# Attention with soft cap, then two MLPs, on one core: a pair's products with v are issued one pair earlier, in PSUM banks of their own

## The chip, the core and the metric

The kernel runs on one core of one Trainium2 chip. The metric is the device time of one execution in microseconds; before the change it is 471.43 us, the median of 3 runs (471.33 to 472.37). Five engines with their own instruction streams work side by side: TensorE (PE in the profile; its weight loads are PEld), VectorE (DVE), ScalarE (ACT), GpSimd (POOL) and SyncE (SP, which issues most DMAs). Each runs its own instructions in the order in which they stand and waits on semaphores for the others.

## The reference

```python
batch, n_heads, seq, head_dim = (2, 12, 448, 64)
n_tokens, d_model, d_ff = (896, 768, 2048)      # first MLP; the second has d_ff 1024

def _attn_ref(q, k, v, cap):
    scores = np.matmul(q, k.transpose(0, 1, 3, 2)) / np.sqrt(q.shape[-1])
    scores = cap * np.tanh(scores / cap)
    scores = scores - np.max(scores, axis=-1, keepdims=True)
    attn = np.exp(scores)
    attn = attn / (np.sum(attn, axis=-1, keepdims=True) + 1e-09)
    return np.matmul(attn, v)

def _moe_ref(x, w_in, w_out, s, b):
    r = np.maximum(x @ w_in, 0.0)
    return (s * (r * r) + b) @ w_out

def _moe2_ref(x, w_in, w_out, g_ln):
    h = x @ w_in
    e = np.exp(h - np.max(h, axis=-1, keepdims=True))
    solu = h * (e / (np.sum(e, axis=-1, keepdims=True) + 1e-09))
    ln = layer_norm(solu) * g_ln
    return ln @ w_out
```

The three follow each other: the output of the attention, 896 tokens by 768, is x of the first MLP, and so on.

## The kernel before

The attention treats the 24 heads as 12 pairs, 0 to 11. All work of a pair n has short names, which stand in the program's order too:

- **pk, pq** (`prep`, lines 418 to 453): TensorE transposes the pair's keys and queries into PSUM. DVE copies the keys to `kh` and makes the rest `kl` (L450, L451); for q it is `qh` and `ql` (L438 or, on ACT, L442, and L443). Each operand of a score is thus split in two, and a product of two split operands is three matmuls (`terms`).
- **s** (`scores_by_key`, L469): scores, transposed, keys on the partitions, in four tiles c = 0 to 3 of a pool `ps_s` with two buffers of two banks. Tiles 0 to 2 hold 128 keys of each head, the last one holds the 64 left over of both. ACT takes tanh of each tile into `e` (L474).
- **exps** (`exps_by_key`, L481): ACT, in two halves: tiles 0 and 1, then 2 and 3.
- **c** (`sums_by_key`, `ends_by_key`): POOL adds up the exponentials of a pair in two adds (L490 after the first half, L493 after the second), then DVE adds the last part in two instructions (L499).
- **o** (`products_by_key`, L511): the product with v, 8 plain float32 matmuls in two halves; the first needs the first half of the exponentials, the second half the rest.
- **m** (`values_by_key`, L521): TensorE sums `c` over the partitions; DVE transposes m (`mt`, L528), inverts it, spreads it (L530, L534), and multiplies o by it (`xf`, L539).
- **split_x**: xf is split again into `xh` and `xl`, the operands of the first MLP: on POOL (L548, L552) for pairs 0 to 9, on ACT and DVE (L199, L200) for pairs 10 and 11.

PSUM has eight banks. While the attention runs, `ps_s` has four of them and the other four are the four buffers of a pool `ps_t`, from which pk, pq, o and m of all pairs take turns.

The order is written out by hand: `then(step, ...)` (line 744) holds each step of the loop in lines 770 to 811 behind the one before it on every engine. Step n of the loop puts on TensorE: s of pair n, tiles 0 and 1; o and m of pair n-2; s of pair n, tiles 2 and 3; pk and pq of pair n+2. The steps of `weights.pump` between them convert the first weights of the MLP (`wt_wi`, L218 to L243, on DVE and ACT), so that DVE has such work in the middle of the attention. DMAs have no place in that order: they are issued by SP in the order in which the program has them, and wait there until what they overwrite is free. The keys, queries and values come in groups of four heads, two pairs; group 0's keys and queries are loaded at the very start, then group 1's, then group 0's v.

After the attention the first MLP begins: `in0_fc` and `in448_fc` are its products for the tokens of the first and of the second batch, from x of pairs 0 to 5 and of pairs 6 to 11. A scheduler mixes the first of these products into the end of the attention.

Of the kernel before, what the change touches and what calls it, by code (L numbers as in the profile page):

```python
# [10 lines left out]
F32 = mybir.dt.float32  # L11
# [26 lines left out]
def tile_softcap_attention__relu2__solu(  # L38
# [20 lines left out]
    P = 128  # L59
# [18 lines left out]
    def psum(name, bufs):  # L78
        return tc.tile_pool(name=name, bufs=bufs, space=PSUM, reuse_waits="tile")
# [4 lines left out]
    def by_query(src, b, heads):  # L84
        return src[b, heads].rearrange("h (p c) d -> p h (c d)", c=NC)
# [4 lines left out]
    def zero_by_key(t, by_pair):  # L90
        for par in range(2):
            threes = (slice(D, P), slice(0, D))[par]
            if by_pair:
                nc.gpsimd.memset(t[threes, :, 3:, par], 0.0)
            else:
                nc.gpsimd.memset(t[threes, par::2, 3 * D:], 0.0)
# [42 lines left out]
    for pr in range(2):  # L139
        pair = slice(2 * pr, 2 * pr + 2)  # L140
# [19 lines left out]
    with psum("ps_w", 1) as ps_w:  # L160
        idle = ps_w.tile([P, 512], F32, name="idle")
# [16 lines left out]
    def layers(ctx, general):  # L178
# [197 lines left out]

        att = ExitStack()
        ps_s = att.enter_context(psum("ps_s", 2))
        ps_t = att.enter_context(psum("ps_t", 3 if general else 4))
        ps_a = att.enter_context(psum("ps_a", 1)) if general else None  # L380
        ap_ = att.enter_context(sb("att", side="right"))

# [3 lines left out]
        def load_group(g, names=("k", "q", "v")):  # L386
            b, i = divmod(g, GB)
            heads = slice(4 * i, 4 * i + 4)
            for nm, src in (("k", k), ("q", q), ("v", v)):
                if nm not in names:  # L390
                    continue
                by_key = nm != "q" and not general
                if g == 0 and (nm == "q" or nm == "k" and by_key):
                    nat[nm, g] = first[nm]
                    continue
                by_pair = nm != "v"
                shape = [P, 2, NC, 2, D] if by_pair else [P, 4, NC * D]
                if by_key:
                    if (nm, g % 3) not in kept:
                        kept[nm, g % 3] = ap_.tile(shape, F32, name=f"{nm}n{g % 3}")  # L400
                        zero_by_key(kept[nm, g % 3], by_pair)
                    t = kept[nm, g % 3]
                    load_by_key(t, src, b, heads, by_pair)
                    nat[nm, g] = t
                    continue
                t = ap_.tile(shape, F32, tag=f"{nm}n", name=f"{nm}n{g}", bufs=3)
                if by_pair:
                    t = t[:CP]
                    load_by_query(t, src, b, heads, nc.gpsimd if g < 2 else None)
                else:  # L410
                    t = t[:CP]
                    nc.sync.dma_start(out=t, in_=by_query(src, b, heads))
                nat[nm, g] = t

        split = {}
        st = {}
# [37 lines left out]

        def terms(n):
            (kh, kl), (qh, ql) = split["k", n], split["q", n]
            return (kh, qh), (kh, ql), (kl, qh)

# [42 lines left out]

        def products_by_key(n, half):
            if half == 0:
                st["o", n] = ps_t.tile([P, 512], F32, tag="t", name=f"o{n}")
            vn = nat["v", n // 2]
            o = st["o", n]
            for c in (2 * half, 2 * half + 1):
                for j in range(2):  # L510
                    nc.tensor.matmul(  # L511
                        o[j * D:(j + 1) * D, :S],
                        lhsT=vn[:, 2 * (n % 2) + j, c * D:(c + 1) * D],
                        rhs=st["e", n][:, 2 * c + j if c < 3 else 6, :],
                        start=(c == 0), stop=(c == NC - 1),
                    )
# [142 lines left out]
        for kk in range(KD):  # L659
            for n in range(2):  # L660
                f = slice(n * HALF, (n + 1) * HALF)
# [43 lines left out]
        for _ in prep(0):  # L705
            pass
        load_group(1, ("k", "q"))
        load_group(0, ("v",))
        if general:
            load_group(2, ("k", "q"))  # L710
            load_small()
            load_group(1, ("v",))
        NPR = NH // 2
        preps = {}

        def prep_half(n):
            if n < NPR:
                if n not in preps:
                    preps[n] = prep(n)
                next(preps[n], 0)  # L720

        if general:
            load_group(2, ("v",))
            for n in range(NPR + 2):
                for c in range(NC):
                    i, c2 = 2 * n + c // 2, c % 2
                    if i < NH:
                        scores(i, c2)
                    if 0 <= i - 1 < NH:
                        exps(i - 1, c2)  # L730
                    if 0 <= i - 2 < NH:
                        transposes(i - 2, 2 * c2)
                        transposes(i - 2, 2 * c2 + 1)
                    if c < 2:
                        prep_half(n + 1)
                if n % 2 == 1 and n // 2 + 3 < NG:
                    load_group(n // 2 + 3)
                if n >= 2:
                    values(n - 2)
        else:  # L740
            last = {}
            traced = nc.cur_bb.bb.instructions

            def then(step, *args):
                with ExitStack() as behind:
                    for ins in last.values():
                        behind.enter_context(tc.issue_after(ins))
                    n = len(traced)
                    step(*args)
                for ins in traced[n:]:  # L750
                    if ins.engine in ordered:
                        last[ins.engine] = ins

            ordered = [e.engine for e in (nc.tensor, nc.vector, nc.scalar, nc.gpsimd)]
            xs["x"] = act_tiles("x")
            idle = ps_t.tile([P, 512], F32, tag="t", name="idle2")
            for n in range(6):
                nc.tensor.matmul(idle[:D, :D], lhsT=ones, rhs=ones, start=True, stop=True)
            then(scores_by_key, 0, 0)
            then(scores_by_key, 0, 1)  # L760
            then(prep_half, 1)
            then(prep_half, 1)
            weights.load(0)
            load_group(2, ("k", "q"))
            load_small()
            load_group(1, ("v",))
            load_group(2, ("v",))
            weights.load(1)
            steps = {1: 3, **{n: 1 for n in range(3, NPR - 2)}, NPR - 2: 2, NPR - 1: 3}
            for n in range(NPR + 2):  # L770
                now = n < NPR
                if now and n > 0:
                    then(scores_by_key, n, 0)
                    then(scores_by_key, n, 1)
                if not now:
                    then(weights.pump, 2)
                if n == 1:
                    then(prep_half, 2)
                    then(prep_half, 2)
                    then(ends_by_key, 0)  # L780
                if n >= 2:
                    then(products_by_key, n - 2, 0)
                    then(products_by_key, n - 2, 1)
                    then(values_by_key, n - 2)
                if now:
                    then(exps_by_key, n, 0)
                if n >= NPR:
                    then(split_x, n - 2)
                elif n >= 3:
                    then(split_x, n - 3)  # L790
                if now:
                    then(sums_by_key, n, 0)
                    then(scores_by_key, n, 2)
                    then(scores_by_key, n, 3)
                    then(exps_by_key, n, 1)
                if 1 < n < NPR:
                    then(ends_by_key, n - 1)
                if n > 0:
                    then(prep_half, n + 2)
                    then(prep_half, n + 2)  # L800
                then(weights.pump, steps.get(n, 0))
                if now:
                    then(sums_by_key, n, 1)
                if n == NPR - 1:
                    then(ends_by_key, n)
                if n == NPR - 1:
                    then(split_x, n - 2)
                if n % 2 == 1 and n // 2 + 3 < NG:
                    load_group(n // 2 + 3, ("k", "q"))
                if n % 2 == 1 and 3 <= (n + 3) // 2 < NG:  # L810
                    load_group((n + 3) // 2, ("v",))
# [129 lines left out]
        for b in range(B):  # L941
            for dc in (2, 3):
                pool, tag = (ps_a, "a") if b == 0 else (ps_b, "b")
# [180 lines left out]
```

## Time and profile before

| what | value |
|---|---|
| time, median of 3 runs | 471.43 us (471.33 to 472.37) |
| the profiled execution's own time | 474.06 us |
| its span, from the first to the last instruction | 472.3 us |
| TensorE busy | 461.2 us, 98% of the span |
| VectorE busy | 346.3 us, 73% |
| ScalarE busy | 273.9 us, 58% |
| GpSimd busy | 92.0 us, 19% |
| mean granted TensorE clock | 0.998 of full speed |

The attention takes about the first 110 us of the span, where GpSimd is busy too. A matmul's end is modelled, so a busy TensorE means that its next instruction was not held up, and not that it runs at its peak. The profiled execution's own time is its span and 1.8 us around it; it lies 2.6 us over the median of the runs.

### The profile page before, as it was taken

To read this page: it belongs to the slowest core of one execution; us is meant where nothing else is said; L and a number is where in the kernel's file an instruction comes from. 1 tells how busy PE (TensorE), PEld (TensorE's weight loads), DVE (VectorE), ACT (ScalarE), POOL (GpSimd) and SP (SyncE) were. 2 spreads that over 40 slices of the span, in tenths; PEclk is the share of its full clock that TensorE was granted. 3 is DMA by queue.
4 is the path that set the end of the run, shared out by engine and by line. 5 is a ranking of instruction groups with operands and counts; after the bars stand their busy time and mean duration, and the time that the engine had idled before them with its cause. 6 is when DMAs were issued, how large, how long until landed. Compare 5 with 4: busy or idle time off the path is not lost.

```text
span 472.3 us, 6596 instructions
## 1 busy us (share of the span) xinstructions
PE 461.2 (98%) x2432; PEld 379.2 (80%) x2432; DVE 346.3 (73%) x564; ACT 273.9 (58%) x394; POOL 92.0 (19%) x91
## 2 busy tenths in 40 slices
PE   7899999999999999999999999999999999999995
PEld 7545564546889898998988889899888898999895
DVE  2699878888698999995699988998958984043110
ACT  2997999871586766765677755555625462033120
POOL 8578878892000000000000000000001110000000
PEclk9999999999999999999999999999999999999999
DMA  8774450204446766532323224444312400011112
GB/s 147 176 196 112 116 161 1 68 0 133 157 116 181 229 211 180 166 111 78 90 85 95 90 90 134 135 133 135 134 67 69 133 1 23 12 33 35 35 35 69
DMA packets 45077, 49.24 MB, mean 104 GB/s; under 512 B 21808, under 2 KB 37296, under 8 KB 45040
## 3 DMA queue, kind: packets, MB, share of 16 engines
q1 hardware_dynamic: 43104, 47.74, 34.9%
q0 software_dynamic: 384, 0.69, 0.8%
q10 hardware_dynamic: 1552, 0.34, 0.4%
q8 instruction: 20, 0.33, 0.3%
q14 instruction: 17, 0.14, 0.1%
HBM read 46.01 MB, written 2.75 MB: 103 GB/s over the span
## 4 chain that ended last, share of the span: by engine, by line
PE 90%; ACT 3%; DVE 3%; DMA 2%; issue 1%; ACTq 0%; SPq 0%; DVEq 0%
PE y L338 8%; PE y L337 8%; PE y L336 8%; PE in L336 7%; PE in L337 7%; PE in L338 7%; PE o L511 7%; PE s L469 7%; PE h L999 4%; PE h L995 4%; PE h L1003 4%; PE o L1046 4%; PE o L1045 4%; PE o L1044 4%; PE m L521 2%; ACT e L474 1%
## 5 line engine op out<-in xcount | busy, mean ns | idle before, releaser
L336 PE MATMUL in<-xh,h_wi 128*128 128x510 f32 (+2 forms) x192 | 70.0, 366 | 0.4 <-ACT xh L199 0.4
L337 PE MATMUL in<-xl,h_wi 128*128 128x510 f32 (+2 forms) x192 | 70.2, 366 | 0.0
L338 PE MATMUL in<-xh,l_wi 128*128 128x510 f32 (+2 forms) x192 | 69.9, 365 | 0.0
L980 POOL TENSOR_SCALAR va<-vs 128x1 f32<-128x1 f32 x7 | 1.8, 254 | 322.3 <-ACT e L979 322.3
L368 ACT ACTIVATE gh<-g,s_t 128x510 fp32r<-128x510 f32 (+1 forms) x64 | 42.2, 668 | 20.1 <-PE y L338 20.0
L369 DVE SCALAR_TENSOR_TENSOR gl<-g,s_t,gh 128x510 fp32r<-128x510 f32 (+1 forms) x64 | 42.8, 681 | 3.4 <-ACT gh L368 3.2
L474 ACT ACTIVATE e<-s 128x896 f32<-128x896 f32 (+1 forms) x48 | 36.9, 818 | 9.0 <-PE s L469 8.9
L481 ACT ACTIVATE e<-e,a_t 128x1792 f32<-128x1792 f32 (+1 forms) x24 | 40.7, 1697 | 0.8
L336 PEld LDWEIGHTS in<-xh,h_wi 128*128 128x128 f32 x192 | 35.9, 187 | 5.9 <-ACT xh L199 0.8
L337 PEld LDWEIGHTS in<-xl,h_wi 128*128 128x128 f32 x192 | 36.0, 188 | 4.7 <-issue 0.7
L338 PEld LDWEIGHTS in<-xh,l_wi 128*128 128x128 f32 x192 | 36.0, 188 | 4.3 <-issue 0.7
L511 PE MATMUL o<-e,vn 128*64 128x448 f32 x192 | 38.7, 545 | 0.0
L1044 PE MATMUL o<-w2o_h,lh 128*128 128x384 f32 (+1 forms) x104 | 35.6, 342 | 0.5 <-ACT lh L199 0.5
L1046 PE MATMUL o<-w2o_h,ll 128*128 128x384 f32 (+1 forms) x104 | 35.4, 342 | 0.0
L1045 PE MATMUL o<-w2o_l,lh 128*128 128x384 f32 (+1 forms) x104 | 35.4, 340 | 0.0
L995 PE MATMUL h<-w2i_h,yh 128*128 128x512 f32 x84 | 33.0, 393 | 0.0
L999 PE MATMUL h<-w2i_l,yh 128*128 128x512 f32 x84 | 33.0, 392 | 0.0
L1003 PE MATMUL h<-w2i_h,yl 128*128 128x512 f32 x84 | 32.8, 390 | 0.0
L511 PEld LDWEIGHTS o<-e,vn 128*64 128x64 f32 x192 | 12.8, 136 | 20.6 <-issue 18.4
L493 POOL TENSOR_TENSOR c<-c,e 128x896 f32<-128x896 f32 x12 | 26.3, 2194 | 13.1 <-ACT e L481 13.1
L199 ACT CAST lh<-x 128x512 fp32r<-128x512 f32 x14 | 7.5, 590 | 35.8 <-PE o L1045 35.5
L490 POOL TENSOR_TENSOR c<-e 128x896 f32<-128x896 f32 x12 | 25.8, 2151 | 7.1 <-ACT e L481 7.1
(426 smaller groups left out, 1111.0 us busy)
## 6 DMA issues: line engine op xcount, KB each, us to landing
raw<-in_moe_w_in_dram SPq DMA_DIRECT2D x16, 768.0 KB, 4.8
raw<-in_moe_w_out_dram SPq DMA_DIRECT2D x24, 512.0 KB, 3.6
raw_w2i<-in_moe_w_in_dram SPq DMA_DIRECT2D x12, 512.0 KB, 3.9
raw<-in_moe_w_out_dram SPq DMA_DIRECT2D x8, 768.0 KB, 4.3
qn<-in_q_dram SPq DMA_DIRECT2D x16, 112.0 KB, 3.0
vn<-in_v_dram SPq DMA_DIRECT2D x12, 128.0 KB, 2.9
kn<-in_k_dram SPq DMA_DIRECT2D x20, 64.0 KB, 3.6
vn<-in_v_dram SPq DMA_DIRECT2D x12, 96.0 KB, 2.6
```

The costliest lines, as they stand in the source:

```text
L336: nc.tensor.matmul(o, lhsT=wh, rhs=xh, start=first, stop=False)
L337: nc.tensor.matmul(o, lhsT=wh, rhs=xl, start=False, stop=False)
L338: nc.tensor.matmul(o, lhsT=wl, rhs=xh, start=False, stop=last)
L368: nc.scalar.mul(out=gh[:, :m], in_=r2, mul=s_t)
L369: nc.vector.scalar_tensor_tensor(out=gl[:, :m], in0=r2, scalar=s_t, in1=full(gh[:, :m]), op0=ALU.mult, op1=ALU.subtract,)
L511: nc.tensor.matmul(o[j * D:(j + 1) * D, :S], lhsT=vn[:, 2 * (n % 2) + j, c * D:(c + 1) * D], rhs=st["e", n][:, 2 * c + j if c < 3 else 6, ...
L995: nc.tensor.matmul(ps[:, n, :], lhsT=yh[:, kk, :], rhs=big["w2i_h"][:, kk, f], start=(kk == 0), stop=False,)
L999: nc.tensor.matmul(ps[:, n, :], lhsT=yh[:, kk, :], rhs=big["w2i_l"][:, kk, f], start=False, stop=False,)
L1003: nc.tensor.matmul(ps[:, n, :], lhsT=yl[:, kk, :], rhs=big["w2i_h"][:, kk, f], start=False, stop=(kk == KD - 1),)
L1044: nc.tensor.matmul(o, lhsT=lh[:, f, :], rhs=wh, start=(f == 0), stop=False)
L1045: nc.tensor.matmul(o, lhsT=lh[:, f, :], rhs=wl, start=False, stop=False)
L1046: nc.tensor.matmul(o, lhsT=ll[:, f, :], rhs=wh, start=False, stop=(f == KF2 - 1))
```

## The change

Four edits. The products with v of pair n-1 (not n-2) are put on TensorE in step n, right behind tiles 0 and 1 of pair n's scores; m and what follows from it stay with pair n-2. The products get a pool `ps_v` with two banks of their own, and `ps_t`, from which pk, pq and m take turns, keeps two. The loads of group 0's v are issued between those of the first and the second pair of group 1's keys. And the second and third matmul of a score change places.

```diff
         ps_s = att.enter_context(psum("ps_s", 2))
-        ps_t = att.enter_context(psum("ps_t", 3 if general else 4))
+        ps_t = att.enter_context(psum("ps_t", 3 if general else 2))
+        ps_v = None if general else att.enter_context(psum("ps_v", 2))
...
                     t = kept[nm, g % 3]
-                    load_by_key(t, src, b, heads, by_pair)
+                    if nm == "k" and g == 1:
+                        for pr in range(2):
+                            pair = slice(heads.start + 2 * pr, heads.start + 2 * pr + 2)
+                            load_by_key(t[:, pr:pr + 1], src, b, pair, by_pair)
+                            if pr == 0:
+                                load_group(0, ("v",))
+                    else:
+                        load_by_key(t, src, b, heads, by_pair)
...
         def terms(n):
             (kh, kl), (qh, ql) = split["k", n], split["q", n]
-            return (kh, qh), (kh, ql), (kl, qh)
+            return (kh, qh), (kl, qh), (kh, ql)
...
         def products_by_key(n, half):
             if half == 0:
-                st["o", n] = ps_t.tile([P, 512], F32, tag="t", name=f"o{n}")
+                st["o", n] = ps_v.tile([P, 512], F32, tag="o", name=f"o{n}")
...
         load_group(1, ("k", "q"))
-        load_group(0, ("v",))
         if general:
+            load_group(0, ("v",))
...
-            idle = ps_t.tile([P, 512], F32, tag="t", name="idle2")
+            idle = ps_v.tile([P, 512], F32, tag="o", name="idle2")
...
+                if 0 < n <= NPR:
+                    then(products_by_key, n - 1, 0)
+                    then(products_by_key, n - 1, 1)
                 if n >= 2:
-                    then(products_by_key, n - 2, 0)
-                    then(products_by_key, n - 2, 1)
                     then(values_by_key, n - 2)
```

`general` is the other arm of the program, for large values of cap, and does not run here. The orders below are the program's, engine by engine. First TensorE in step 1, with the number of the pair in each name (pk2 is pair 2's pk, s1_2 is tile 2 of pair 1); before:

```order
L427 MATMUL pk2_300<-ident_62,kn1_163 128x128 x4
L427 MATMUL pq2_309<-ident_62,qn1_174 128x112 x4
L469 MATMUL s1_2_323<-qh1_226,kh1_217 128x448 x2
L469 MATMUL s1_2_323<-ql1_227,kh1_217 128x448 x2
L469 MATMUL s1_2_323<-qh1_226,kl1_218 128x448 x2
L469 MATMUL s1_3_331<-qh1_226,kh1_217 128x448
L469 MATMUL s1_3_331<-ql1_227,kh1_217 128x448
L469 MATMUL s1_3_331<-qh1_226,kl1_218 128x448
L427 MATMUL pk3_337<-ident_62,kn1_163 128x128 x4
```

And the same place of the changed program:

```order
L435 MATMUL pk2_303<-ident_62,kn1_166 128x128 x4
L435 MATMUL pq2_312<-ident_62,qn1_184 128x112 x4
L519 MATMUL o0_323<-e0_198,vn0_173 64x448 x8
L477 MATMUL s1_2_335<-qh1_229,kh1_220 128x448 x2
L477 MATMUL s1_2_335<-qh1_229,kl1_221 128x448 x2
L477 MATMUL s1_2_335<-ql1_230,kh1_220 128x448 x2
L477 MATMUL s1_3_343<-qh1_229,kh1_220 128x448
L477 MATMUL s1_3_343<-qh1_229,kl1_221 128x448
L477 MATMUL s1_3_343<-ql1_230,kh1_220 128x448
L435 MATMUL pk3_349<-ident_62,kn1_166 128x128 x4
```

The 8 products of pair 0 stand in front of pair 1's last two score tiles; before, they stood behind tiles 0 and 1 of pair 2. In each later step up to pair 11 the order is that of before, with o of the next pair in o's place. Next TensorE behind the last score tile of the last pair; before:

```order
L469 MATMUL s11_3_1154<-qh11_1037,kh11_1028 128x448
L469 MATMUL s11_3_1154<-ql11_1038,kh11_1028 128x448
L469 MATMUL s11_3_1154<-qh11_1037,kl11_1029 128x448
L511 MATMUL o10_1178<-e10_1043,vn2_257 64x448 x8
L336 MATMUL in0_0_1263<-xh_186,h_wi0_355 128x448
```

And now:

```order
L477 MATMUL s11_3_1166<-qh11_1049,kh11_1040 128x448
L477 MATMUL s11_3_1166<-qh11_1049,kl11_1041 128x448
L477 MATMUL s11_3_1166<-ql11_1050,kh11_1040 128x448
L519 MATMUL o11_1190<-e11_1116,vn2_260 64x448 x4
L336 MATMUL in0_0_1267<-xh_189,h_wi0_367 128x448
```

Pair 10's products are over before this place, and only one pair's are left for the stretch behind it. Last SP, from the first load of group 1's keys (kn1) on; before:

```order
L112 DMA kn1_163<-in_k_dram 64x4x64 x2
L112 DMA kn1_163<-in_k_dram 64x3x64 x2
L112 DMA kn1_163<-in_k_dram 64x4x64 x2
L112 DMA kn1_163<-in_k_dram 64x3x64 x2
L117 DMA vn0_179<-in_v_dram 64x2x256
L117 DMA vn0_179<-in_v_dram 64x2x192
L117 DMA vn0_179<-in_v_dram 64x2x256
L117 DMA vn0_179<-in_v_dram 64x2x192
```

And now:

```order
L112 DMA kn1_166<-in_k_dram 64x4x64
L112 DMA kn1_166<-in_k_dram 64x3x64
L112 DMA kn1_166<-in_k_dram 64x4x64
L112 DMA kn1_166<-in_k_dram 64x3x64
L117 DMA vn0_173<-in_v_dram 64x2x256
L117 DMA vn0_173<-in_v_dram 64x2x192
L117 DMA vn0_173<-in_v_dram 64x2x256
L117 DMA vn0_173<-in_v_dram 64x2x192
L112 DMA kn1_166<-in_k_dram 64x4x64
```

The four loads of v come four loads earlier, and those of the second pair's keys four later. On VectorE and GpSimd's compute the order is the same through the whole attention and its end, up to the split of pair 11; on ScalarE it is the same up to there too.

## Rows read from the trace of the kernel before

**Rows 1.** The page's first part: busy us, share of the span, instructions.

```profile
PE 461.2 (98%) x2432; PEld 379.2 (80%) x2432; DVE 346.3 (73%) x564; ACT 273.9 (58%) x394; POOL 92.0 (19%) x91
```

**Rows 2.** Waits of PE: line, what ended them; total us, times, longest.

```profile
PE s L469 <- ACT e L474: 2.5, 4, 1.0
PE in L336 <- ACT xh L199: 0.4, 1, 0.4
```

**Rows 3.** Chain that ended last, in order of time: start us, us, what.

```profile
86.92 3.16 PE o L511 x16
...
98.89 1.36 ACT e L474 x2
...
102.63 2.29 DVE wt_wi L223
...
110.77 4.87 DMA raw<-in_moe_w_in_dram
...
122.74 0.57 ACT xh L199
123.36 0.68 PE in L336 x2
```

**Rows 4.** Timeline of PE: start us, us, engine, line, operation, count [idle before <-releaser].

```profile
18.21 0.55 PE L427 MATMUL pq<-ident,qn 112*128 112x112 f32 x4
19.06 0.47 PE L469 MATMUL s<-qh,kh 64*128 64x448 f32 x2 [0.31 <-ACT e L474]
...
22.59 0.47 PE L469 MATMUL s<-qh,kh 64*128 64x448 f32 x2 [1.02 <-ACT e L474]
...
27.07 0.92 PE L521 MATMUL m<-c,ones 128*64 128x448 f32 x4
27.92 0.47 PE L469 MATMUL s<-qh,kh 64*128 64x448 f32 x2
...
29.87 0.55 PE L427 MATMUL pq<-ident,qn 112*128 112x112 f32 x4
...
34.83 1.55 PE L521 MATMUL m<-c,ones 128*64 128x448 f32 x4
36.31 0.47 PE L469 MATMUL s<-qh,kh 64*128 64x448 f32 x2
...
84.94 0.55 PE L427 MATMUL pq<-ident,qn 112*128 112x112 f32 x4
```

**Rows 5.** DMA issues of v, and their timeline on SP.

```profile
vn<-in_v_dram SPq DMA_DIRECT2D x12, 128.0 KB, 2.9
...
11.37 2.56 SPq L117 DMA_DIRECT2D vn<-in_v_dram  x4
```

**Rows 6.** Timeline of ACT.

```profile
21.64 1.33 ACT L474 ACTIVATE e<-s 128x896 f32<-128x896 f32 x2
...
26.16 1.88 ACT L481 ACTIVATE e<-e,a_t 128x1792 f32<-128x1792 f32 x1
28.83 1.35 ACT L474 ACTIVATE e<-s 128x896 f32<-128x896 f32 x2 [0.79 <-PE s L469]
```

**Rows 7.** Timeline of POOL: the two adds of pair 2.

```profile
28.12 2.22 POOL L490 TENSOR_TENSOR c<-e 128x896 f32<-128x896 f32 x1 [1.35 <-ACT e L481]
31.88 2.10 POOL L493 TENSOR_TENSOR c<-c,e 128x896 f32<-128x896 f32 x1 [1.53 <-ACT e L481]
```

**Rows 8.** Timeline of DVE.

```profile
28.41 2.75 DVE L232 SCALAR_TENSOR_TENSOR wt_wi<-raw,wt_wi 128x768 uint32<-128x768 uint32 x1
31.08 0.64 DVE L528 STREAM_TRANSPOSE mt<-m 128x448 f32<-128x448 f32 x1
...
33.25 2.11 DVE L499 SCALAR_TENSOR_TENSOR c<-c,e 64x448 f32<-64x448 f32 x2
...
36.12 0.69 DVE L451 TENSOR_TENSOR kl<-pk,kh 128x512 fp32r<-128x512 f32 x1
...
83.11 0.65 DVE L528 STREAM_TRANSPOSE mt<-m 128x448 f32<-128x448 f32 x1 [1.03 <-PE m L521]
```

## The prediction

> **What bounds the kernel now.** I read the busy shares first: TensorE is busy 98% of the span [rows 1], so a gain has to come out of its few waits or out of its work, and the change leaves its work as it is. The list of its waits comes next: for score tiles it waits 2.5 us in four places, each time for the tanh that frees a bank, and once, 0.4 us, for xh of the last pair [rows 2]. The timeline of TensorE shows where: of the four, 0.31 us stands ahead of pair 1's tile 2 and 1.02 us ahead of pair 2's tile 0 [rows 4]. The other two cannot be reached: one lies ahead of pair 1's tile 0, where no exponentials are complete yet, the other ahead of pair 11.
>
> The chain of waits tells the rest. From 22.59 us on it runs along TensorE, pair after pair, until the last pair's tile 2. There it leaves TensorE: from 98.89 us it goes over tanh and exp of pair 11 on ACT to the weight conversion on DVE, a weight DMA that waits for that conversion, more of DVE, and xh of pair 11 on ACT; TensorE comes back at 123.36 us, with the first MLP's products of pair 11's tokens [rows 3]. In these 24.5 us TensorE had work enough for all but 0.4 us [rows 2], but none of it is in the chain. So there are two stretches with different limits: up to pair 11's scores TensorE's work decides, and behind them the chain over ACT and DVE, which starts when these scores are done.
>
> **The change part by part.** I follow pair 1 to pair 3 with the durations of the trace; the sum goes against the profiled execution, 474.06 us (span 472.3), which lies 2.6 us over the median of 471.43; I carry the difference over to the median.
>
> *o of pair 0 moves up, into step 1.* It may start behind pq2, at 18.21 + 0.55 = 18.76 [rows 4]. Its exponentials are there: on ACT they stand in front of the tanh whose end released TensorE at 19.06. Its v is there too: in the trace the four loads were issued from 11.37 to 13.93 and such a load lands after 2.9 us [rows 5], by about 16.8 even without the earlier place; the keys that now come later are used at about 23. An o that is followed by other work takes 3.16 us [rows 3]. So pair 1's tile 2 starts at 18.76 + 3.16 = 21.92 instead of 19.06.
>
> *What it fills and what it delays.* tanh of that tile follows 0.91 us after its start (27.92 and 28.83 in the next pair [rows 4, 6]), at 22.83. Before it began at 21.64, held up by ACT alone, so ACT falls back by 1.19 us, and with it all it does without a gap until 28.04, the end of the first half of pair 2's exponentials [rows 6]: now 29.23. TensorE goes on without waiting: from a tile 2 to the m of the next step it needs 34.83 - 27.92 = 6.91 us, and m takes 0.85 until the next tile 2 [rows 4]. m of pair 0 comes at 28.83, pair 2's tile 2 at 29.68, where it was 27.92. Of 3.16 us of added work 1.40 us are regained here, the waits of 0.31 and 1.02 and a rest.
>
> *Two banks for pk, pq and m.* They take turns in the order pk, pq, m. So pq of pair 4 gets the bank of m of pair 0, and must wait for its transpose mt on DVE; before, four banks kept them apart. pq4 could start 1.95 us behind tile 2 [rows 4], at 31.63. mt of pair 0 ended at 31.72 before, although m was there at 28: DVE was in the weight step L232, 2.75 us long, and that was held up by POOL's add [rows 7, 8]. The add starts when the exponentials of pair 2 are half done, so all of it moves with ACT by 1.19 us: mt ends at 32.91. TensorE waits 1.28 us.
>
> *m behind kl.* m of pair 1 now has the bank of pk4, so it waits for kl4 on DVE, not only for c1 as before. From pq4 to m1 it is 4.96 us [rows 4]: 37.87. c1 on DVE began at 33.25 and ended 1.38 us after POOL's second add of pair 2, at 35.36; kl4 ended 1.45 us later [rows 7, 8]. That add follows tanh of pair 2's tile 2, which moves from 28.83 to 29.68 + 0.91 = 30.59, by 1.76: it ends at 35.74, c1 at 37.12, kl4 at 38.57. TensorE waits 0.75 us with the semaphore, and pair 3's tile 2 starts at 39.47. Before it was 36.31, with 0.63 us of waiting for c1 in it (m took 1.55 instead of 0.92 us). The sum is 3.16 - 1.40 - 0.63 + 1.28 + 0.75 = 3.16 us: what the early o fills, the narrower pool gives back.
>
> Neither wait shows in the trace, so I bound the two together: nothing, if DVE is on time (TensorE is then 3.16 - 1.40 - 0.63 = 1.13 us late), and 2.0 us as worked out. I take the latter, since its terms are four rows that all move with ACT.
>
> *Later pairs.* mt of a later pair ends at 83.76, and TensorE's pq of that step starts at 84.94: 1.2 us to spare. DVE stood idle 1.03 us before that mt [rows 4, 8], so kl was done by m's start as well. An o follows the xf of two pairs earlier, which ends 2.2 us behind mt's start (31.08 to 33.25), at 85.3, before the o of 86.92 [rows 3, 8]. Its second half needs the exponentials of its own pair, which ACT finishes ahead of the next pair's tanh. So no wait repeats, and the period stays. Order of the terms: the same three matmuls; nothing. The loads of v: hidden as shown, and no queue behind them is late.
>
> *The end.* TensorE reaches the last pair's scores 3.16 us later, having done one o more. From there the chain over ACT and DVE has the same members in the same order and takes the same 24.5 us. TensorE has one o less to do beside it, so it waits 0.43 + 3.16 = 3.6 us there, instead of 0.4: the work that was moved out of this stretch had cost nothing in it. Behind 123.36 us the chain is TensorE again without a gap that could take up 3 us. Sum: 474.06 + 3.16 = 477.2 for a profiled execution, 474.6 us for the median.
>
> **The rivals.** *TensorE's work decides everywhere* (faster). Then the order of the work is of no account and only its waits count: 0.31 + 1.02 + 0.63 = 1.96 us go, 469.5 us; with the new waits of 2.0 us added it is 471.5, no change. For it: TensorE is busy 98%. Against it: the chain of 24.5 us without TensorE in it, which would have to become 3 us shorter. This is also the way of the Trainium skill, Perfetto Trace Analysis, sections Identifying the Most-Contended Engine and Optimization Strategy: take the engine with the highest occupancy, find its gaps and make the dependencies behind them start sooner. By it the change is a gain of the 1.96 us; the same section speaks of regimes that change over time, and the trace bears that out, with the chain's 24.5 us.
>
> *DVE gets ahead of POOL* (slower, but less). L232 began 0.29 us behind POOL's add and lasted 2.75 us [rows 7, 8]. If it starts first, it need not wait until the add ends at 30.34, which is 1.93 us behind its start. mt, c1 and kl4 come in time and both waits vanish: 1.13 us, 472.6. Against it: both sides move with ACT. The Trainium skill, SBUF — State Buffer, section Who interferes with whom, says that the engine that issues first holds the shared port pair for its whole instruction and the other blocks fully. By that rule 0.3 us decide over these 2 us; the row's 2.75 us fit it.
>
> *v is late*, so that o of pair 0 does not do what it is there for: each us by which v lands behind 18.76 delays TensorE by as much; with 1.2 us it is 475.8. Against it: 2 us to spare.
>
> **How the numbers follow.** The forecast, 474.6, has 0.66, with 473.6 to 475.6 as its own range (a third of the unknown waits either way). DVE ahead of POOL, 472.6: 0.13. TensorE's work decides: 0.18, of which 0.10 at 469.5 and 0.08 at no change. v late: 0.03. A measurement of this kernel tells about 0.2%, 0.94 us, from no change. Faster 0.10, same 0.08, slower 0.82. The range, 471.3 to 475.8 us, takes in all but the 0.10 and the tails.
>
> **What would show it.** In the changed profile: o of pair 0 at about 18.8, pair 1's tile 2 near 21.9 with no wait ahead of it or of pair 2's tile 0; a wait of about 1.3 us ahead of pq in the step of pair 2, released by mt, and one of 0.7 us ahead of the next m, released by kl; the last pair's tile 2 some 3 us later than 98; a wait for xh of over 3 us, with a shorter one for xl of pair 10 ahead of it, in the first MLP's first products. The prediction is wrong if that last wait stays near 0.4 us, or if pair 11's scores come no later than before.

## The result: 476.6 us, slower by about 1%, and the profile after

The changed kernel takes 476.63 us, the median of 6 runs (474.62 to 477.06), against 471.40 us, now the median of 6 runs (471.33 to 472.37). The ratio is 1.0096, with a 95% interval of 1.0080 to 1.0112: slower by 4.5 us by the ratio, 5.2 by the medians. Direction and mechanism are those of the forecast; its 474.6 us and its range, which ended at 475.8, are too low. The profiled execution of the changed kernel, 474.62 us with a span of 472.8, was the shortest of the six; three of the others have a lower mean granted clock, 0.994 to 0.995 instead of 0.998. The longest, 477.06 us, has 0.998 too.

First the page's busy shares and then the list of TensorE's waits (line, what ended them; total us, times, longest), to be read against [rows 1, 2]:

```profile
PE 458.9 (97%) x2432; PEld 377.1 (80%) x2432; DVE 345.2 (73%) x564; ACT 274.5 (58%) x394; POOL 92.0 (19%) x91
```

```profile
PE in L336 <- ACT xh L199: 2.5, 1, 2.5
PE s L477 <- ACT e L482: 1.6, 2, 1.3
PE pq L435 <- DVE mt L536: 1.2, 1, 1.2
...
PE o L519 <- DVE xf L547: 0.9, 1, 0.9
...
PE m L529 <- DVE kl L459: 0.5, 1, 0.5
```

Two of the four waits for tanh are gone, as they should be; three new ones stand in the list, pq for mt, m for kl and o for xf, and the wait for xh has grown from 0.4 to 2.5 us. The timeline of TensorE shows their places (start us, us, engine, line, operation, idle before and what ended it):

```profile
7.91 0.47 PE L477 MATMUL s<-qh,kh 64*128 64x448 f32 x2
...
16.25 3.23 PE L519 MATMUL o<-e,vn 128*64 128x448 f32 x16
19.41 0.47 PE L477 MATMUL s<-qh,kh 64*128 64x448 f32 x2
...
21.84 0.47 PE L477 MATMUL s<-qh,kh 64*128 64x448 f32 x2
...
30.52 0.60 PE L435 MATMUL pq<-ident,qn 112*128 112x112 f32 x4 [1.24 <-DVE mt L536]
...
36.20 0.97 PE L529 MATMUL m<-c,ones 128*64 128x448 f32 x4 [0.50 <-DVE kl L459]
...
100.06 0.37 PE L477 MATMUL s<-ql,kh 128*128 128x448 f32 x1
...
101.38 1.72 PE L519 MATMUL o<-e,vn 128*64 128x448 f32 x8 [0.94 <-DVE xf L547]
...
123.97 0.68 PE L336 MATMUL in<-xh,h_wi 128*128 128x448 f32 x2 [2.47 <-ACT xh L199]
```

All of this starts earlier than in the trace of before, and that does not come from the change: in e8 (below), whose program is that of before up to the last pair's scores, the first score starts at 8.05 us. Two rows of before, its first score and the last matmul of the last pair's scores:

```profile
9.94 0.74 PE L469 MATMUL s<-qh,kh 64*128 64x448 f32 x2
...
99.29 0.37 PE L469 MATMUL s<-qh,kl 128*128 128x448 f32 x1
```

The first score starts at 9.94 in the one trace and at 7.91 in the other, and its matmul takes 0.74 us in the one and 0.47 in the other: TensorE waited 1.60 us instead of 0.62 for the first keys, and it ran slower, although the granted clock on record there is 1.00 in both traces. Fourteen traces of this study have that start between 7.76 and 9.94, and kernels whose TensorE work is the same up to 100 us differ in it too (7.91 to 8.00 in three traces of the changed kernel, 9.07 to 9.48 in e5, e6 and e10 below). So I cut each span in three and compare the parts: up to the first score; from there to the start of the last matmul of the last pair's scores; the rest. The experiment in which only the order of the terms and the loads changed (e12, below) stands in for the kernel before with an early start. Its first score and the last matmul of the last pair's scores:

```profile
7.90 0.47 PE L476 MATMUL s<-qh,kh 64*128 64x448 f32 x2
...
96.48 0.37 PE L476 MATMUL s<-ql,kh 128*128 128x448 f32 x1
```

| kernel | first score at | to the last score | the rest of the span |
|---|---|---|---|
| before | 9.94 | 89.35 | 372.98 |
| terms and loads alone (e12) | 7.90 | 88.58 | 372.93 |
| changed | 7.91 | 92.15 | 372.76 |
| changed, second trace (e1) | 7.93 | 91.94 | 374.14 |
| changed, third trace (e9) | 8.00 | 91.81 | 374.19 |

The middle part has grown by 3.2 to 3.6 us (by 2.9 to 3.3 against e8's 88.88), and the rest, in which one o less has to be done, has not become shorter. That is the forecast. In two of three traces the rest is 1.4 us longer still. That is what it missed.

The chain of waits of the changed kernel (start us, us, what) shows why the rest stayed:

```profile
99.67 1.36 ACT e L482 x2
...
103.40 2.29 DVE wt_wi L223
...
111.56 4.70 DMA raw<-in_moe_w_in_dram
...
122.70 0.64 DVE xf L547
123.97 0.68 PE in L336 x2
```

From 99.67 to 123.97 it is 24.3 us, with the members of before, where it was 24.5 [rows 3].

### The profile page after: what moved, and what is told of

Same layout as the page of the kernel before. It is cut to its first block, busy times and chain, and to the rows that moved or that the text cites. A ratio compares the mean times of both kernels' runs of the same rounds, so it can differ in the third digit from the quotient of the medians.

```text
span 472.8 us, 6602 instructions
## 1 busy us (share of the span) xinstructions
PE 458.9 (97%) x2432; PEld 377.1 (80%) x2432; DVE 345.2 (73%) x564; ACT 274.5 (58%) x394; POOL 92.0 (19%) x91
## 4 chain that ended last, share of the span: by engine, by line
PE 86%; DVE 5%; SPq 3%; DMA 2%; ACT 1%; issue 1%; ACTq 0%; DVEq 0%
PE y L338 8%; PE y L337 8%; PE y L336 8%; PE in L336 7%; PE in L337 7%; PE in L338 7%; PE o L519 5%; PE s L477 5%; PE h L1004 4%; PE h L1008 4%; PE h L1012 4%; PE o L1054 4%; PE o L1055 4%; PE o L1053 4%; SPq L112 3%; PE m L529 1%
```

## The experiments

Twelve experiments ran, in three sessions of four. In each session the kernel before ran beside them: 471.80 us (18 runs), 472.03 (28) and 471.51 (17).

**e1, the changed kernel again.**

> The changed kernel once more, unaltered, for a second trace and more times. Two theories stand for the time it takes beyond 471.4 us. Theory 1 (the last pair): 3.2 us, because one o more stands ahead of the last pair's scores and the chain behind them over ACT and DVE keeps its 24 us; 474.6 us, and what single runs have above that comes from the first 13 us, where the first keys' landing and TensorE's speed differ from run to run; the trace then shows the same 3 us of waits for xl and xh in the first MLP's first products, and in a run of 476 to 477 us the first score tile 2 us later than at 7.9 us. Theory 2 (lost speed): the longer wait of TensorE in the first MLP's first products is followed by matmuls at a lower granted clock, 2 us beside the 3.2, so that 476.6 us is the rule; the trace then shows a granted clock below 1.0 behind 120 us and the first score tile where it was.

476.36 us (475.80 to 477.00), ratio 1.0096 (1.0077 to 1.0114). All six runs have a mean clock of 0.994 to 0.996. Busy time by stretch, with the granted clock (PEclk) behind the engines, first of the trace of the result, then of e1:

```profile
122.00:130.00 8.00, 6.03 (x28) 5.24 (x29) 4.52 (x7) 6.30 (x12) 0.00 (x0) 1.00 0.69 229
```

```profile
122.00:130.00 8.00, 6.31 (x22) 5.41 (x23) 4.33 (x8) 6.32 (x12) 0.00 (x0) 0.79 0.73 229
130.00:140.00 10.00, 10.00 (x50) 8.89 (x49) 8.76 (x14) 7.74 (x15) 0.00 (x0) 1.00 0.33 100
```

In e1's timeline the fall stands right behind the wait for xh:

```profile
120.74 0.36 PE L337 MATMUL in<-xl,h_wi 128*128 128x448 f32 x1
120.94 0.37 PE L338 MATMUL in<-xh,l_wi 128*128 128x448 f32 x1
123.69 0.67 PE L336 MATMUL in<-xh,h_wi 128*128 128x448 f32 x2 [2.38 <-ACT xh L199]
124.35 0.74 PE L337 MATMUL in<-xl,h_wi 128*128 128x448 f32 x1
124.89 0.57 PE L338 MATMUL in<-xh,l_wi 128*128 128x448 f32 x1
125.26 0.57 PE L337 MATMUL in<-xl,h_wi 128*128 128x448 f32 x1
```

The last of these starts 0.37 us behind the one before it, as do those that follow up to 127.5 us, and not 0.20 as ahead of the wait: the lower of the two levels, 1.2 instead of 2.4 GHz. The first score is at 7.93, so theory 1's explanation by the beginning fails for this run and theory 2's holds. The 1.00 of the trace of the result says that the same wait, 2.47 us there, need not have that effect.

**e2, the banks alone.** Only this differs from the changed kernel:

```diff
-                if 0 < n <= NPR:
-                    then(products_by_key, n - 1, 0)
-                    then(products_by_key, n - 1, 1)
                 if n >= 2:
+                    then(products_by_key, n - 2, 0)
+                    then(products_by_key, n - 2, 1)
                     then(values_by_key, n - 2)
```

> The changed kernel with the products of pair n-2 in step n, as before the change; the two pools of two banks, the order of the terms and the place of v's loads stay changed. Theory 1: of the 3.2 us the part of the banks alone stays: pq of pair 4 waits for mt of pair 0 (31.7 us in the trace of before, against 29.9), some 1.9 us, and m of pair 1 for kl of pair 4 with c's own wait in it, so some 1.2 to 1.9 us of delay reach the last pair's scores; the holes of 0.31 and 1.02 us stay. 472.6 to 473.3 us, the wait for xh of pair 11 between 1.5 and 2.5 us. Rival (the early products alone cost): 471.4. Theory 2 expects 471.4 or 472.6 as well, but without a longer wait no clock below 1.0.

474.29 us (473.11 to 476.02), ratio 1.0056 (1.0035 to 1.0078), above the expectation. In the trace pq waits for mt as reckoned:

```profile
30.74 0.60 PE L435 MATMUL pq<-ident,qn 112*128 112x112 f32 x4 [1.73 <-DVE mt L536]
```

The part up to the last score is 89.84 us, 1.26 more than e12's, and the rest 372.88. The wait for xh stayed at 0.49: here TensorE and the chain are late by the same amount, and my 1.5 to 2.5 us were wrong. Four of its seven runs have a mean clock of 0.990 to 0.994; the profiled one, at 0.998, does not show where, so their cause is open, and with it about half of the 2.5 us by which this kernel is slower.

**e3 and e4, the last two products late again.** In both, the products of pairs 10 and 11 go back; in e4 a DVE step moves too (the last two lines of the diff):

```diff
-                if 0 < n <= NPR:
-                    then(products_by_key, n - 1, 0)
-                    then(products_by_key, n - 1, 1)
+                if n != 0 and n != NPR - 1:
+                    late = n - 1 if n < NPR else n - 2
+                    then(products_by_key, late, 0)
+                    then(products_by_key, late, 1)
...
-            steps = {1: 3, **{n: 1 for n in range(3, NPR - 2)}, NPR - 2: 2, NPR - 1: 3}
+            steps = {1: 2, 2: 1, **{n: 1 for n in range(3, NPR - 2)}, NPR - 2: 2, NPR - 1: 3}
```

> The changed kernel, but the products of pairs 10 and 11 stay two steps behind: step 11 holds no o, steps 12 and 13 hold those of pairs 10 and 11 as before the change. Theory 1: the last pair's tile 2 comes 3.16 us earlier than in the changed kernel, the chain behind it is unchanged, TensorE's wait for xh of pair 11 falls from over 3 us to about 0.4, and the time to 471.4 us (the holes filled at the beginning, 1.96 us with m's, and the two new waits, 2.0 us, cancel). Rival (the work on TensorE decides, wherever it stands): no change from the changed kernel, 474.6 to 476.6. Theory 2 agrees with theory 1 here and adds that all runs have the same clock as before.

> As the run before it, and the third of three weight steps that step 1 puts on DVE (L232) moves behind step 2's work, so that mt of pair 0, c of pair 1 and kl of pair 4 no longer stand behind it. Theory 1: the waits ahead of pq of pair 4 and of m of pair 1 vanish, 2.0 us, and the last pair's scores come 2 us earlier; TensorE then has no wait left but those ahead of pair 1 and pair 11: 469.3 to 469.8 us. Rival (the waits come from the banks whatever stands on DVE): 471.4.

e3: 475.57 us (474.15 to 477.04), ratio 1.0073 (1.0050 to 1.0096); e4: 473.37 us (472.15 to 473.89), 1.0027 (1.0015 to 1.0039). Both expectations are missed, and e3's trace says why:

```profile
102.12 0.97 PE L529 MATMUL m<-c,ones 128*64 128x448 f32 x2 [0.86 <-DVE c L507]
104.62 1.01 PE L529 MATMUL m<-c,ones 128*64 128x448 f32 x1 [1.54 <-DVE c L507]
```

The scores come earlier (89.98 us to the last one), but the scheduler now puts m of pair 10 ahead of the first MLP's first products, where it waits for c with nothing in front of it; in e3's profile, not in e4's, the granted clock is one half behind that, too, up to 108 us. So this pair of runs does not test the chain: I had changed what stands behind the scores as well. It does show the DVE step: in e4 the waits ahead of pq and of m of pair 1 are gone, 87.83 instead of 89.98 us to the last score, 2.15 us for the 2.0 reckoned.

**e5 and e10, two microseconds of useless work.**

```diff
+                if tok.start == S and fc == 0 and kk == KD - 2 and not general:
+                    extra = ps_y.tile([P, 512], F32, tag="y", name="extra")
+                    for _ in range(10):
+                        nc.tensor.matmul(
+                            extra[:, :m], lhsT=wl[:, kk * P:(kk + 1) * P], rhs=xl[:, kk, tok],
+                            start=True, stop=True,
+                        )
```

> The changed kernel with 10 useless matmuls (some 2 us of work for TensorE, into a PSUM bank of their own, from operands that are there) just ahead of the first product that needs xh of pair 11, where TensorE waits 2.4 us. Theory 1 with theory 2 (the chain over ACT and DVE sets the end of this stretch, and the idle TensorE is given the lower clock behind it): the work costs nothing, the wait for xh falls to about 0.4 us, the mean granted clock is 0.998 in every run instead of 0.994 to 0.996 in most, and the time falls by 1 to 1.5 us, to about 475 (474.4 to 475.4). Theory 1 alone (the clock has other reasons): no change, 476.4, with the same clocks. Rival (TensorE's work decides): slower by 2 us, 478.4.

> The changed kernel with the 10 useless matmuls in the wait for xh once more, since only four of its runs counted and its profiled run lost clock at the beginning. 2a: no stretch at the lower clock between 100 and 140 us, since the wait there is 0.45 us; the median 0.5 to 1.5 us below the run before it. 2b: the same median as the run before it.

e5: 476.12 us (476.05 to 476.27, 4 runs), 1.0089 (1.0074 to 1.0105); e10, with the changed kernel (e9) beside it in the same session: 474.96 us (474.22 to 475.67), 1.0065 (1.0045 to 1.0084). In e10's trace:

```profile
122.28 2.19 PE L355 MATMUL extra<-xl,l_wi 128*128 128x448 f32 x10
124.93 0.68 PE L336 MATMUL in<-xh,h_wi 128*128 128x448 f32 x2 [0.46 <-ACT xh L199]
```

```profile
122.00:130.00 8.00, 7.54 (x37) 6.34 (x36) 4.96 (x8) 5.69 (x11) 0.00 (x0) 1.00 0.70 231
```

The work costs nothing: the rest of the span is 372.67 us (372.85 in e5) against 372.76. In neither trace does the clock fall here, and no run of e10 has a mean below 0.997. e10 lies 1.1 us under e9. e5's time did not fall as expected. Its profiled run lost time at the beginning, where the first score starts at 9.10 us and the granted clock fell before it; but its two runs with a mean clock of 0.999 and 1.000 took 476.05 and 476.27 us, no less, and why is open. So what the lower clock costs is shown by the last parts of the traces; the times of e9 and e10, whose intervals overlap, agree with it and do not prove it.

**e9, the changed kernel a third time.**

> The changed kernel, unaltered, a third trace, beside the two runs that follow. Two theories of what it costs beyond the 3.2 us of the forecast: theory 2a, the lower clock behind the wait for xh (2.4 us), seen in one of its two traces so far (3.4 us at half the clock, 1.4 us lost); theory 2b, the beginning alone (first keys' landing and the clock there), which differs between runs and has nothing to do with the change. 2a: a granted clock of 0.5 for 3.4 us right behind that wait, and 476.4 us; 2b: no such stretch, 476.4 us with the first score at 9 us or later.

476.03 us (474.62 to 477.70), 1.0073 to 1.0122. First score at 8.00, a wait of 2.46 us for xh, and 0.79 of the clock from 122 to 130 us: theory 2a again, in five of six runs by their mean clock.

```profile
122.00:130.00 8.00, 6.02 (x23) 5.38 (x24) 4.26 (x7) 5.94 (x12) 0.00 (x0) 0.79 0.68 229
```

**e11, a longer chain.**

```diff
-            nc.vector.transpose(out=turned, in_=m[:, :S])
+            for _ in range(4 if n == NPR - 1 else 1):
+                nc.vector.transpose(out=turned, in_=m[:, :S])
```

> The changed kernel with three more transposes of m of pair 11 on DVE (0.64 us each, the same result written again), which stand in the chain ahead of xf of pair 11. Chain theory: TensorE's wait for xh grows from 2.4 by 1.95 to 4.3 us and the time by 1.95 us. 2a: the longer wait is followed by the lower clock in every run (mean clock 0.996 or less), so that the time is 478.4 us (476.4 + 1.95) or a little more, since now no run escapes. 2b: 478.4 us, with the clock as it was. Rival (the chain doesn't set the end): 476.4.

478.58 us (477.82 to 479.51), ratio 1.0144 (1.0122 to 1.0167), 2.55 us over e9. The wait, and the clock behind it:

```profile
126.00 1.11 PE L336 MATMUL in<-xh,h_wi 128*128 128x448 f32 x2 [4.53 <-ACT xh L199]
```

```profile
122.00:130.00 8.00, 4.00 (x11) 3.53 (x12) 4.69 (x8) 3.92 (x8) 0.00 (x0) 0.63 0.70 229
130.00:140.00 10.00, 10.00 (x47) 8.85 (x46) 9.41 (x16) 9.02 (x17) 0.00 (x0) 0.95 0.15 53
```

Three DVE instructions of 0.64 us, far off TensorE's busy time, delay the kernel by their full length. All runs have 0.991 to 0.994. The rest of the span is 376.88 us, 4.12 more than in the trace of the result: 2.06 of longer wait, and 2.06 behind it, where the clock is lower.

**e6, e7 and e8, a shorter chain.** The conversion of the weights wi4 goes behind the split of pair 11; in e7 beside that the DVE step of e4 moves; e8 is the kernel before with the first of the two.

```diff
-                weights.pump(1)
+                if general or weights.done != 4:
+                    weights.pump(1)
+                else:
+                    then(weights.pump, 1)
```

> The changed kernel, but the conversion of weights wi4 (with its weight DMA ahead of it in the chain) is put behind the split of pair 11 on DVE and ACT, so that xf and xh of pair 11 don't wait for it. Theory 1: xh of pair 11 comes 3 us or more earlier, TensorE's wait of 2.4 us ahead of it goes, the last pair's scores come as late as in the changed kernel: 476.4 - 2.5 = 473.9 us, and with theory 2, whose cost of 1.3 us goes with the wait, 472.6 (472.0 to 473.0). Rival (the last pair's lateness itself costs the time, or something behind 130 us): no change, 476.4.

> The run before it and, beside that, the third weight step of step 1 on DVE moved behind step 2's work, which took away the waits ahead of pq of pair 4 and of m of pair 1 in an earlier run. Theory 1 with theory 2: 1.7 us less than the run before it, 470.9 us (470.4 to 471.4), somewhat less than before the change, since all of TensorE's holes behind pair 1 are closed. Rival (the waits at the banks are made good later): as the run before it.

> The kernel before the change with the same shortening of the chain at the end of the attention as in the two runs before this one. Theory 1: TensorE waited 0.43 us there, so 0.4 us less, 471.2 us, and about as much as with the early products, if these only fill what the narrower pool gives back. Theory 2 adds that runs with a granted clock of 0.994, 1 us longer, become fewer if that short wait set them off, and stay if they come from elsewhere.

| | time, us | ratio (95%) | first score | to the last score | the rest |
|---|---|---|---|---|---|
| e6 | 471.49 (471.16 to 473.02) | 0.9995 (0.9983 to 1.0006) | 9.07 | 91.82 | 369.83 |
| e7 | 469.59 (468.79 to 471.91) | 0.9950 (0.9935 to 0.9965) | 9.83 | 89.35 | 369.63 |
| e8 | 470.70 (470.06 to 471.46) | 0.9975 (0.9965 to 0.9985) | 8.05 | 88.88 | 372.24 |

In e6 xf of pair 11 starts at 120.08 on DVE (122.70 in the changed kernel), and the wait for xh is gone:

```profile
118.38 0.64 DVE L536 STREAM_TRANSPOSE mt<-m 128x448 f32<-128x448 f32 x1
...
120.08 0.62 DVE L547 TENSOR_TENSOR xf<-o,rs 128x448 f32<-128x448 f32 x1
...
122.15 0.56 DVE L223 TENSOR_SCALAR wt_wi<-wt_wi 128x768 f32<-128x768 f32 x1 [0.19 <-ACT wt_wi L222]
```

The last pair's scores are as late as in the changed kernel, and the rest is 2.9 us shorter. No run of the three kernels has a mean clock below 0.997, 33 runs in all. The medians are 0.5 to 1.3 us lower than expected (472.6, 470.9 and 471.2); why is open. In e7's timeline nothing waits at the two banks any more:

```profile
30.15 0.60 PE L435 MATMUL pk<-ident,kn 128*128 128x128 f32 x4
30.58 0.55 PE L435 MATMUL pq<-ident,qn 112*128 112x112 f32 x4
...
35.53 0.92 PE L529 MATMUL m<-c,ones 128*64 128x448 f32 x4
```

e7 beats both kernels, and e8 by 1.1 us. But e8 keeps the DVE step L232 in its old place, ahead of the c for which m waited 0.63 us before. So e7 shows what the early products, the banks and the moved step give together; what the early products alone are worth is not shown.

**e12, the two small parts alone**, on the kernel before: order of the terms and place of v's loads, as in the diff of the change.

> The kernel before the change with only the two small parts of it: the second and third matmul of a score in the other order, and group 0's v loaded between the pairs of group 1's keys. All theories: no difference, since neither the same three matmuls nor loads that land 2 us early decide anything: within 0.2% of the kernel before, 471.0 to 472.9 us. If it is slower by 1 us or more, part of what was put down to the clock and the beginning belongs to these parts.

472.23 us (471.16 to 473.05), ratio 1.0007 (0.9993 to 1.0021): no difference.

## What of the prediction was right, and which step failed

- **o of pair 0 fills the holes: right.** It starts at 16.25, with the earlier start of that trace (2.03 us) at 18.28 for 18.76; pair 1's tile 2 and pair 2's tile 0 have no wait any more.
- **Two banks give it back: right.** pq waits 1.24 us for mt (reckoned 1.28), m 0.50 us for kl (0.75). e7 shows the reason given, DVE's step L232: with that moved the same banks make nobody wait. So the rival with DVE ahead of POOL (472.6) did not happen, and v was not late.
- **3.16 us up to the last scores: right**, 3.2 to 3.6 measured against e12, 2.9 to 3.3 against e8.
- **The chain of 24.5 us sets the end: right.** It took 24.3 us. TensorE's 3.6 us of waiting came as 2.47 for xh and 0.94 for xf of pair 9, where I had named xl of pair 10. e10 (2.2 us of work for nothing), e11 (2 us on DVE for 2 us and more) and e6 (chain shortened, time back) show it from three sides. The rival that TensorE's work decides everywhere falls with e10. Of the Trainium skill's way (Perfetto Trace Analysis, section Optimization Strategy: find the busiest engine's gaps and let what they wait for start sooner) the change took only the finding, and filled the gaps with work from elsewhere. e6 lets xh start sooner, and the traces agree with that way: the wait is gone and the rest is 2.9 us shorter.
- **Failed: "the work that was moved out of this stretch had cost nothing in it", and 3.16 us as the whole price of the wait.** That work had kept TensorE busy until its operands came. Without it TensorE stands still for 2.4 us and mostly comes back at half its clock, 1.4 us more (374.14 or 374.19 against 372.76). Before the change the wait was 0.43 us [rows 2], so no row showed the fall, but I priced a wait by its length alone: the sum has no term for the matmuls behind it. 471.4 + 3.2 + 1.4 is 476.0, within the runs' spread; in the sessions of e1 and e9 the changed kernel is 4.6 and 4.5 us over the kernel before, which is 3.2 and 1.4, while of the 5.2 us of the result 0.6 stay open. The Trainium skill, TensorE: Matmul & The Clock Gate, section Why this matters for your kernels, warns of idle gaps of TensorE between bursts of matmuls, but of longer ones than this. Here 2.4 us had that effect in two of three traces, and the measurement decides.
- **Also too narrow: the beginning.** First scores from 7.76 to 9.94 us and a spread of up to 3 us in the runs of one kernel were not in the range, though the 2.6 us between the profiled execution and the median hinted at it. For a profiled execution the forecast was 477.2 us; the one of the result took 474.62, mainly because its first score came 2.03 us earlier.

What stays open: some runs of the kernel before (8 of the 63 beside the experiments) have a mean clock of 0.993 to 0.996 as well, and no trace shows where; what sets the start of the first score; why e5 was not shorter than the changed kernel; and what decides whether a wait of 2.4 us brings the clock down.

## What to carry to other kernels

Ask of work that is to move what it covers where it stands now: taken out of a stretch that a chain over other engines ends, it saves nothing there and leaves the busiest engine idle. Price a new wait of TensorE at its length and at what it runs slower behind it. Where such a chain exists, shorten it first (here, weight conversions that could wait stood ahead of the last pair's operands); the kernel with the early products beat the one before only after that.

## What was new about the hardware

A wait of TensorE of 2.4 us was followed by a granted clock of one half in two of three traces (1.4 us lost), one of 4.5 us in the one trace there is (2.06 us), and one of 0.43 to 0.51 us in none of the five traces that have it (before, e2, e5, e10 and e12). Two shorter ones close together, 0.86 and 1.54 us with 1 us of matmuls between them, were followed by it in e3's trace, and not in e4's, which has the same pair.
